# Attention with beacon keys, then a soft mixture of experts: the last 80 keys two to a partition, a 64-row product first, second-layer weights in 8 KB rows, column halves at the end

## The chip, the cores and the metric

The kernel runs on one core of one Trainium2 chip. The metric is the device time of one execution in microseconds; the time of a kernel is the median of several runs. A profile is one further execution, recorded by the hardware profiler, with a time of its own. Engines are named as in the profile: PE (matrix products; PEld is its weight load), DVE (VectorE), ACT (ScalarE), POOL (GpSimd) and SP (SyncE, which here only issues transfers).

## What is computed

Attention over 8 x 8 heads with 576 tokens, 16 beacon keys ahead of them and 64 columns a head, then a soft mixture of 8 experts with 4 slots each over all 4608 tokens:

```python
k_all = concatenate([beacon_k, k], axis=2)          # 16 + 576 = 592 keys
v_all = concatenate([beacon_v, v], axis=2)
scores = q @ k_all^T / sqrt(64), later tokens masked
a = exp(scores) / sum(exp(scores))
x = (a @ v_all) as [4608 tokens, 512]
logits = x @ phi                                    # 32 slots
d = softmax of logits over the tokens;  slot_input = d.T @ x
for e in range(8):
    h = maximum(slot_input[e] @ w1[e], 0)           # 512 -> 1024
    slot_out[e] = h @ w2[e]                         # 1024 -> 512
c = softmax of logits over the slots;   out = c @ slot_out
```

All inputs and the output are float32. q, k and v are 9.4 MB each, w1 and w2 16.8 MB each, the output 9.4 MB.

## The kernel before

**Pairs.** The 64 heads are worked on two at a time: 32 pairs, `n` from 0 to 31, four pairs a batch `b`, with `g = n % 4`. One quad of heads (two pairs) of q and k is loaded by `load_quad` (L88) and transposed by `transp` (L236). The order of all instructions is written out by hand; each engine takes its own in that order.

**Keys.** The 592 keys are five blocks. For the first four (R = 0, 1; two blocks each), two neighbouring keys stand on one partition (r = 0, 1). The last 80 keys stand one to a partition.

**Steps of a pair.** `score(n, st)` (L251) makes scores on PE and their exponentials on ACT in four steps, into two PSUM tiles in turn:
- step 0: the 64-key triangles of both R, 64-row products with both heads at once in the two halves of the array; one exponential of 512 columns (L272); POOL zeroes what lies above the diagonal (L275, two of 64x512)
- steps 1 and 2: keys r = 0 and 1 of R = 0 against all later tokens, a mask added by a product (L263), an exponential of 928 columns (L284)
- step 3: the keys of R = 1 against later tokens, then the last 80 keys against the last 80 tokens (80x80), one exponential of 992 columns (L295), and POOL zeroes above the diagonal of the 80x80 part (L296)

Between the steps of pair `n` stand the products with V of pair `n - 1`: `attend_sh` (L308, the triangles: 64 rows) and `attend` (L319, whole blocks, L335; for token block 4 these load 80 columns of weights, and the last 80 keys are a product of their own, L331). `norm` (L338) divides by the row sums, which come out of a column of ones beside V. `pop` takes pieces of the routing work of the batch before (`routing`: transposes of x, logits, slot inputs) according to `slots`.

**V.** `load_v` (L105) loads V in three parts and the beacons' V: keys two to a partition in rows of 512 B, the last 80 in rows of 256 B (L115), and for b > 0 the beacons' V into a tile of its own (L120). `cast_v` casts to f16: on POOL L356 (and L361 for the beacons), on DVE L359 for the last 80. `lift_v` (L364) copies the second head of each pair to partitions 64 to 127 on DVE (L367), for `attend_sh`.

**Weights.** `load_w` (L131) loads 32 pieces of 256 or 512 rows with a cast from float32 to f16, issued by POOL. 22 have a place of their own, 10 reuse tiles of q, k and V. `want(n)` says how many are issued by the end of pair `n`: 0.68 a pair up to 22, then 1.8; the rest at the end of the last pair. A w1 piece has 8 KB rows in memory, a w2 piece 4 KB rows.

**The end.** After the last pair: logits and slot inputs of the last batch, `layer1` for two groups of experts, `sums` (36 small products for the row sums of c), `turn`, `layer2` for eight experts (L642, 512 columns, four column groups at once), the scaling of the slot outputs by DVE (`soh`, L657), and then nine groups of 512 tokens: product (L669), eviction by ACT (L671) and DVE (L674) in turn, and transfers of 512 KB (L676).

SP issues all loads of q, k, v, phi and the beacons' keys and the output in one order; POOL issues the weights between its masks and casts.

Of the kernel before, what the change touches and what calls it, by code (L numbers as in the profile page):

```python
# [17 lines left out]
def kernel(  # L18
# [43 lines left out]
    SH, S0, S1, S2 = 0, 512, 512 + 928, 512 + 2 * 928  # L62
    EW = S2 + 992

    def ecol(a, i, R, r):
        if i == 2 * R:
            return None
        if R == 0:
            return (S0, S1)[r] + 464 * a + P * i - P
        return S2 + 496 * a + 208 * r + P * i - 3 * P  # L70
# [5 lines left out]
    vbp = ctx.enter_context(tc.tile_pool(name="vbp", bufs=1))  # L76
# [3 lines left out]
    wh = ctx.enter_context(tc.tile_pool(name="wh", bufs=NW))  # L80
# [7 lines left out]
    def load_quad(m):  # L88
        b, qd = divmod(m, QH)
        for (d, src, nm) in ((qf, q, "qf"), (kf, k, "kf")):  # L90
            d[m] = qkp.tile([P, 2, J, D], FP, name=nm, tag=nm)
            for x in range(2):
                h0 = 4 * qd + 2 * x
                nc.sync.dma_start(
                    out=d[m][:, x, :, :],
                    in_=src[b, h0:h0 + 2].rearrange("h s d -> (h s) d").rearrange(
                        "(p j) d -> p j d", j=J))
# [7 lines left out]
    def load_v(b, what):  # L105
        base = b * H * S - Nb
        if what in (0, 1):
            t = vf[(b, what)] = vfp.tile([P, H, 2 * D], FP, name="vf", tag="vf")
            if what == 0 and b == 0:
                nc.sync.dma_start(out=t[Nb // 2:P], in_=vpairs(base + Nb, P - Nb // 2, 2))  # L110
            else:
                nc.sync.dma_start(out=t[:, :, :], in_=vpairs(base + 2 * P * what, P, 2))
        elif what == 2:
            t = vf[(b, 2)] = vlp.tile([P, H, D], FP, name="vl", tag="vl")
            nc.sync.dma_start(out=t[0:UL], in_=vpairs(base + 4 * P, UL, 1))  # L115
        else:
            t = vf.get((0, 0))
            if b > 0:
                t = vf[(b, 3)] = vbp.tile([P, H, 2 * D], FP, name="vb", tag="vb")
            nc.sync.dma_start(  # L120
                out=t[0:Nb // 2],
                in_=beacon_v[b].rearrange("h (n r) d -> n h (r d)", r=2))
# [3 lines left out]
    homes = ["vf", "vf", "qf", "kf", "vf", "vb", "qf", "kf", "qf", "kf"][:NPC - NW]  # L126
    assert len(homes) == NPC - NW

    pieces = [(e, r) for e in range(E) for r in (0, 1)] + [(e, r) for e in range(E) for r in (2, 3)]

    def load_w(m):  # L131
        if m < NW:
# [517 lines left out]
    for e in range(4):  # L650
        layer2(e)
# [55 lines left out]
```

## Time and profile before

| | us |
|---|---|
| median of 3 runs (211.12 to 211.56) | 211.18 |
| the profiled execution | 211.68 |
| its span, first to last instruction | 209.9 |
| busy: PE / DVE / ACT / POOL | 171.2 / 131.2 / 131.4 / 102.7 |
| last products of the last pair | about 165 |
| last weights used | 180.06 |
| first output transfer issued | 182.81 |

The granted TensorE clock was 0.96 on average. The profile's page gives busy shares in 40 slices of the span (5.25 us each), in tenths. A group line gives source line, engine, operation, tiles written and read, shapes and count; then the busy time and the mean of one in ns; then the engine's idle time just before and what ended it. A line of waits gives who waited for whom, the total, the number of times and the longest. A line of a stretch gives from:to, its length, and for PE, PEld, DVE, ACT and POOL the busy time and the number of instructions, then the granted clock, the DMA share and GB/s. In the timeline a line begins with start and duration.

### The profile page before, as it was taken

The numbers are of one execution on the slowest core, as the hardware profiler recorded it, in microseconds if no ns is written. First come the engines' busy times: TensorE is split into PE (matmuls) and PEld (weight loads), VectorE is DVE, ScalarE is ACT, GpSimd is POOL, SyncE is SP. The second block draws the span as 40 slices with busy tenths as digits, with TensorE's granted clock in tenths as the row PEclk, the third lists the DMA queues.
The fourth block names the chain that finished last, engine by engine and source line by source line (L and its number), as shares of the span: only waits on it lengthen the run. The fifth ranks groups of instructions, "written<-read, shape, count | busy, mean of one in ns | idle before, by whom it ended". The sixth has DMA issues, their size and how long they took to land.

```text
span 209.9 us, 7327 instructions
## 1 busy us (share of the span) xinstructions
PE 171.2 (82%) x3168; PEld 118.7 (57%) x3168; DVE 131.2 (63%) x255; ACT 131.4 (63%) x186; POOL 102.7 (49%) x181
## 2 busy tenths in 40 slices
PE   2569789799999989989999998997998799687000
PEld 2346567576776767667677776765766656232000
DVE  3324479876985987698588769857644523499000
ACT  2373569598679858867967886795596440398000
POOL 3054268349646843973694478579567620000000
PEclk9999999999999999999999999998799999999755
DMA  6999999999999999999999999999999998099994
GB/s 193 218 267 370 335 288 324 244 274 290 296 241 311 343 238 301 338 261 262 294 285 231 310 305 262 209 210 184 203 170 183 212 211 164 6 404 401 408 404 186
DMA packets 42463, 55.82 MB, mean 266 GB/s; under 512 B 8959, under 2 KB 25791, under 8 KB 42431
## 3 DMA queue, kind: packets, MB, share of 16 engines
q1 hardware_dynamic: 35775, 38.58, 59.1%
q0 software_dynamic: 6656, 16.78, 42.5%
q8 instruction: 25, 0.41, 0.8%
q14 instruction: 7, 0.06, 0.1%
HBM read 62.69 MB, written 9.44 MB: 344 GB/s over the span
## 4 chain that ended last, share of the span: by engine, by line
PE 45%; DVE 24%; DMA 10%; issue 4%; POOL 3%; SPq 3%; ACT 2%; DVEq 0%; POOLq 0%
PE av L335 13%; PE sc L259 12%; PE tr L244 7%; DMA wx<-in_moe_w_dram 6%; DVE xb L348 6%; DVE qT L245 5%; DVE vh L359 4%; DMA vl<-in_v_dram 4%; PE tr L387 4%; DVE vu L367 3%; DVE osb L674 3%; PE av L316 3%; PE tr L402 3%; PE sc L263 2%; ACT ex L284 1%
## 5 line engine op out<-in xcount | busy, mean ns | idle before, releaser
L284 ACT ACTIVATE ex<-sc 128x928 f16<-128x928 f32 x64 | 59.7, 943 | 29.3 <-PE sc L263 29.0
L259 PE MATMUL sc<-qT,kT 64*64 64x128 bf16 (+3 forms) x576 | 55.2, 267 | 3.0 <-POOL kT L232 1.4
L275 POOL TENSOR_SCALAR_AFFINE_SELECT ex<-ex 64x512 f16<-64x512 f16 x64 | 42.6, 665 | 5.9 <-ACT ex L272 3.4
L335 PE MATMUL av<-vh,ex 128*128 128x65 f16 (+1 forms) x756 | 42.6, 201 | 0.0
L335 PEld LDWEIGHTS <-ex 128*128 128x128 f16 (+1 forms) x768 | 32.2, 108 | 17.4 <-issue 15.7
L295 ACT ACTIVATE ex<-sc 128x992 f16<-128x992 f32 x32 | 31.9, 997 | 4.9 <-PE sc L259 4.7
L296 POOL TENSOR_SCALAR_AFFINE_SELECT ex<-ex 80x160 f16<-80x160 f16 x32 | 10.6, 330 | 49.8 <-ACT ex L295 49.0
L259 PEld LDWEIGHTS <-kT 64*64 64x64 bf16 (+2 forms) x576 | 25.2, 104 | 16.2 <-issue 4.7
L245 DVE COPY kT<-tr 128x640 bf16<-128x640 bf16 (+1 forms) x31 | 23.9, 775 | 7.4 <-PE tr L244 7.4
L263 PE MATMUL sc<-mk,low 64*128 64x128 bf16 x256 | 26.8, 224 | 0.0
L348 DVE TENSOR_TENSOR xb<-av,r 128x640 f16<-128x640 f32 (+1 forms) x32 | 26.0, 814 | 1.1
L245 DVE COPY qT<-tr 128x640 bf16<-128x640 bf16 (+1 forms) x31 | 23.7, 771 | 4.2 <-PE tr L244 3.8
L272 ACT ACTIVATE ex<-sc 128x512 f16<-128x512 f32 x32 | 19.0, 593 | 5.9 <-PE sc L259 5.2
L346 DVE RECIPROCAL r<-av 128x10 f32<-128x10 f32 (+1 forms) x32 | 7.0, 218 | 23.7 <-PE av L331 22.7
L244 PE MATMUL tr<-idb,qf 128*64 128x128 bf16 x288 | 14.9, 236 | 4.0 <-DMA qf<-in_q_dram 4.0
L244 PE MATMUL tr<-idb,kf 128*64 128x128 bf16 x288 | 15.0, 235 | 2.9 <-DVE qT L245 1.9
L671 ACT ACTIVATE osb<-fp,rc 128x512 f32<-128x512 f32 x18 | 11.3, 687 | 9.4 <-PE fp L669 8.7
L356 POOL CAST vh<-vf 128x1024 f16<-128x1024 f32 x15 | 15.7, 1048 | 0.6 <-DMA vf<-in_v_dram 0.6
L146 POOL DMA_DIRECT2D w<-in_moe_w_dram x22 | 13.2, 601 | 0.7
L244 PEld LDWEIGHTS <-qf 128*64 128x64 bf16 x288 | 9.9, 117 | 6.3 <-DMA qf<-in_q_dram 4.2
L316 PE MATMUL av<-vh,ex 64*128 64x65 f16 x128 | 10.4, 194 | 3.5 <-DVE xb L348 2.8
L244 PEld LDWEIGHTS <-kf 128*64 128x64 bf16 x288 | 10.3, 117 | 5.0 <-DMA kf<-in_k_dram 1.4
(96 smaller groups left out, 232.5 us busy)
## 6 DMA issues: line engine op xcount, KB each, us to landing
w<-in_moe_w_dram POOLq DMA_DIRECT2D x22, 512.0 KB, 8.3
qf<-in_q_dram SPq DMA_DIRECT2D x32, 288.0 KB, 7.3
kf<-in_k_dram SPq DMA_DIRECT2D x32, 288.0 KB, 7.1
out_dram<-osb SPq DMA_DIRECT2D x18, 512.0 KB, 6.3
vf<-in_v_dram SPq DMA_DIRECT2D x15, 512.0 KB, 10.9
wx<-in_moe_w_dram POOLq DMA_DIRECT2D x10, 512.0 KB, 10.3
vl<-in_v_dram SPq DMA_DIRECT2D x8, 160.0 KB, 11.3
vf<-in_v_dram SPq DMA_DIRECT2D x1, 480.0 KB, 8.2
```

The source lines that it names most:

```text
L244: nc.tensor.transpose(tp[64 * x:64 * x + 64, j - j0, :], hi, idb[:, :])
L245: (nc.scalar.copy if act else nc.vector.tensor_copy)(out=dst[:, :, Nb:U].rearrange("p y (s j) -> p y s j", j=J)[:, :, :, j0:j1], in_=tp[:, ...
L259: nc.tensor.matmul(out, kt[64 * a:64 * a + 64, lhs], qt[64 * a:64 * a + 64, rhs], start=True, stop=stop)
L263: nc.tensor.matmul(out, low[64 * a:64 * a + 64, :], mk[64 * a:64 * a + 64, r, :], start=False, stop=True)
L272: nc.scalar.activation(e[:, SH:SH + 512], sc[:, 0, :], AF.Exp, scale=scale)
L275: nc.gpsimd.affine_select(out=ap, in_=ap, compare_op=AL.is_ge, fill=0.0, base=0, pattern=[[0, 2], [-1, 2], [1, P]], channel_multiplier=-2)
L284: nc.scalar.activation(e[:, o:o + 928].rearrange("p (a t) -> p a t", a=2), sc[:, :, 0:464], AF.Exp, scale=scale)
L295: nc.scalar.activation(ev, sc[:, :, 0:496], AF.Exp, scale=scale)
L316: nc.tensor.matmul(avout(n, a, 2 * R), e[64 * a:64 * a + 64, c:c + P], rhs, start=(r == 0), stop=(R == 0 and r == 1))
L335: nc.tensor.matmul(avout(n, a, i), e[:, c:c + m], vh[b % 2][:, 2 * x[0] + x[1], h, :], start=(z == 0 and i != 2), stop=(z == len(L) - 1))
L348: nc.vector.tensor_tensor(out=xo, in0=avv[:, :, :, 0:D], in1=r5[:, 0:w, :].unsqueeze(3).broadcast_to([P, w, NCH, D]), op=AL.mult)
L356: eng.tensor_copy(out=w[:, 2 * what:2 * what + 2, :, 0:D].rearrange("p r h d -> p h r d"), in_=t[:, :, :].rearrange("p h (r d) -> p h r d" ...
```

## The change

- The last 80 keys of each head stand two to a partition, on 40 partitions. Their scores move from step 3 to step 0, where they lie behind the triangles (672 instead of 512 columns); their mask is added by a product. Step 3's exponential has 832 instead of 992 columns, and L296 is gone. With V they are a second part of `attend_sh` (R = 2).
- For token block 4 the products load 128 columns of weights (the tile of exponentials has 48 zero columns at its end).
- The first part of `attend_sh` stands straight behind step 0, the rest of pair n - 1 behind steps 1 and 2; pair 0's products with V all stand behind pair 1's scores.
- V's lifts read the loaded float32 tile, and stand on POOL (on DVE for batch 0); the casts of a batch stand one pair earlier, and V is loaded one step earlier. The beacons' V is loaded into the tile that it belongs to. A quad of q or k is one transfer from the second quad on, the beacons' keys come in 2 KB rows, and the first loads are in another order.
- A w2 piece has 8 KB rows in memory. The last three pieces are loaded in two column halves each, all first halves before the second ones (35 requests). `want` is 0.70 a pair up to 26, then 2.2.
- `layer2` works on 256 columns at a time. After the first halves of the last pieces, the first 256 columns are joined, multiplied out and written for two groups of tokens; then the second halves. The other seven groups follow in transfers of 1 MB. 24 of the 36 sums are made within the loop.

```diff
-    SH, S0, S1, S2 = 0, 512, 512 + 928, 512 + 2 * 928
-    EW = S2 + 992
+    SH, S0, S1, S2 = 0, 672, 672 + 928, 672 + 2 * 928
+    EW = S2 + 832 + 48
+    K2 = UL // 2
...
+            for x in ((0, 1) if m == 0 else (slice(0, 2),)):
+                nc.sync.dma_start(out=t[:, x], in_=s4[:, x])
...
+    def load_v(b, R):
+        base = b * H * S - Nb + 2 * P * R
+        if R < 2:
+            t = vfp.tile([P, H, 2 * D], FP, name="vf", tag="vf")
+            lo = Nb // 2 if R == 0 else 0
+            nc.sync.dma_start(out=t[lo:P], in_=vpairs(base + 2 * lo, P - lo, 2))
+            if R == 0:
+                nc.sync.dma_start(out=t[0:lo],
+                                  in_=beacon_v[b].rearrange("h (n r) d -> n h (r d)", r=2))
         else:
+            t = vlp.tile([K2, H, 2 * D], FP, name="vl", tag="vl")
+            nc.sync.dma_start(out=t[:, :, :], in_=vpairs(base, K2, 2))
+        vf[(b, R)] = t
...
+    XH = 3
+    halved = pieces[NPC - XH:]
+    reqs = ([(p_, None) for p_ in pieces[:NPC - XH]] + [(p_, 0) for p_ in halved]
+            + [(p_, 1) for p_ in halved])
...
+            src = moe_w2[e, (r - 2) * 512:(r - 1) * 512].rearrange("(p s) d -> p s d", p=P)
+            if hf is None:
+                src = src.rearrange("p s d -> p (s d)")
+            else:
+                src = src[:, :, 256 * hf:256 * hf + 256]
...
     load_quad(0)
...
     load_v(0, 0)
-    load_v(0, 3)
+    load_quad(1)
     load_v(0, 1)
     load_v(0, 2)
+    load_quad(2)
     phif = const.tile([P, NDC, NSL], FP, name="phif")
...
+            for r in range(2):
+                c = 512 + UL * r
+                for a in range(2):
+                    mm(a, fl[64 * a:64 * a + K2, c:c + UL], slice(512 + r, U, 2), slice(512, U), False)
+                for a in range(2):
+                    mm_mask(a, r, fl[64 * a:64 * a + K2, c:c + UL],
+                            idb[64 * a:64 * a + 64, 64 * a:64 * a + K2])
+            nc.scalar.activation(e[:, 0:S0], fl[:, 0:S0], AF.Exp, scale=scale)
...
+    def attend_sh(n, Rs, heads2=(0, 1)):
...
+            kn = 64 if R < 2 else K2
             for r in range(2):
+                c = P * (2 * R + r) if R < 2 else 512 + UL * r
+                for a in heads2:
+                    if a == 0 and R < 2:
+                        rhs = vh[b % 2][0:64, 2 * R + r, ha, :]
+                    else:
+                        rhs = vu[b % 2][64 * a:64 * a + kn, R, g, r, :]
...
+    def by_pair(t):
+        return t.rearrange("p (Q x y) c -> p Q x (y c)", Q=QH, x=2)
...
+    def lift_v(b, R, x, eng):
+        t = vf[(b, R)]
+        kn = 64 if R < 2 else K2
+        eng.tensor_copy(
+            out=vu[b % 2][64 * x:64 * x + kn, R, :, :, 0:D].rearrange(
+                "p (Q y) r d -> p Q (y r) d", Q=QH),
+            in_=by_pair(t[0:kn])[:, :, x, :].rearrange("p Q (y d) -> p Q y d", d=D))
...
-        return int(0.68 * min(n, 22) + 1.8 * max(0, n - 22))
+        return int(0.70 * min(n, 26) + 2.2 * max(0, n - 26))
...
+    def turns(n, part):
+        m, w = (n // 2 + 1, 1 - part) if n % 2 == 0 else ((n + 3 - 2 * part) // 2, part)
+        if m < NQ:
+            transp(m, w, part)
...
+    def whole(n):
+        attend_sh(n, (0, 1))
+        for a in range(2):
+            attend(n, a, (2, 1, 3, 4))
+        attend_sh(n, (2,))
+        norm(n)
...
         score(n, 0)
+        if n >= 2:
+            attend_sh(n - 1, (0, 1))
...
         score(n, 1)
...
+            attend(n - 1, 0, (2,))
+            attend(n - 1, 1, (2,))
+            attend(n - 1, 0, (1, 3, 4))
+        if n > 2:
+            turns(n, 1)
...
         score(n, 2)
...
+        if n >= 2:
+            attend(n - 1, 1, (1, 3, 4))
...
+            attend_sh(n - 1, (2,))
             norm(n - 1)
...
+            if g == 1:
+                cast_v(b + 1, 0, nc.gpsimd)
+                lift_v(b + 1, 0, 1, nc.gpsimd)
+            if g == 2:
+                cast_v(b + 1, 1, nc.gpsimd)
+                lift_v(b + 1, 1, 1, nc.gpsimd)
+            if g == 3:
+                lift_v(b + 1, 2, 0, nc.gpsimd)
+                lift_v(b + 1, 2, 1, nc.gpsimd)
...
+    def layer2(e, r, hf):
+        for t in range(4 * (r - 2), 4 * (r - 1)):
             c = t % 4
+            nc.tensor.matmul(sop[hf][32 * c:32 * c + 32, :], hTz[:, t, NSL * e:NSL * e + NSL],
+                             w2c(e, t, hf), start=(e == 0 and t < 4), stop=(e == E - 1 and t >= 4))
...
+    def join(hf):
+        w = slice(256 * hf, 256 * hf + 256)
+        if hf == 0:
+            nc.vector.tensor_scalar(out=soh[:, w], in0=sop[hf], scalar1=rd[:, 0:1],
+                                    scalar2=None, op0=AL.mult)
+        else:
+            nc.scalar.activation(soh[:, w], sop[hf], AF.Copy, scale=rd[:, 0:1])
...
+    def rows(cg, j, osb, w, fp_):
+        i = cg * G + j
+        nc.tensor.matmul(fp_[:, w], etok(cg, j), soh[:, w], start=True, stop=True)
+        if j % 2 == 0:
+            nc.scalar.activation(osb[:, j, w], fp_[:, w], AF.Copy, scale=rc[:, i:i + 1])
+        else:
+            nc.vector.tensor_scalar(out=osb[:, j, w], in0=fp_[:, w], scalar1=rc[:, i:i + 1],
+                                    scalar2=None, op0=AL.mult)
...
+    for (e, r) in halved:
+        layer2(e, r, 0)
+    join(0)
+    w = slice(0, 256)
+    for cg in range(NLG):
+        for j in range(G):
+            rows(cg, j, osbs[cg], w, ps_tr.tile([P, Dm], FP, name="tr", tag="tr"))
+            if j % 2:
+                nc.sync.dma_start(out=dst(cg)[:, j - 1:j + 1, w], in_=osbs[cg][:, j - 1:j + 1, w])
+    for (e, r) in halved:
+        layer2(e, r, 1)
+    join(1)
...
+    w = slice(0, Dm)
+    for cg in range(NLG, NG):
+        osb = wh.tile([P, G, Dm], FP, name="osb", tag="w")
+        for j in range(G):
+            rows(cg, j, osb, w, ps_f.tile([P, Dm], FP, name="fp", tag="fp"))
+        nc.sync.dma_start(out=dst(cg), in_=osb[:, :, :])
```

## The prediction

> **What bounds the kernel now.** I read the page's slices first, then its DMA queues, then ten-microsecond stretches, the timeline of the end, the waits, and the groups.
>
> ```profile
> PE   2569789799999989989999998997998799687000
> DMA  6999999999999999999999999999999998099994
> GB/s 193 218 267 370 335 288 324 244 274 290 296 241 311 343 238 301 338 261 262 294 285 231 310 305 262 209 210 184 203 170 183 212 211 164 6 404 401 408 404 186
> ...
> q1 hardware_dynamic: 35775, 38.58, 59.1%
> q0 software_dynamic: 6656, 16.78, 42.5%
> ...
> HBM read 62.69 MB, written 9.44 MB: 344 GB/s over the span
> ```
>
> The DMA row stands at 9 from the second slice to the 33rd, falls to 0 in the 35th (179 to 184 us), and is full again until the output is out. The queues' packets took 59.1 + 42.5 = 101.6% of sixteen engines' span. The weights' queue (q0) counts what it writes in f16; it reads twice that.
>
> ```profile
> 130.00:140.00 10.00, 10.00 (x205) 7.13 (x205) 7.62 (x13) 7.48 (x11) 6.68 (x14) 1.00 1.09 209
> 140.00:150.00 10.00, 8.62 (x161) 6.21 (x161) 5.74 (x15) 6.11 (x9) 7.91 (x11) 0.83 1.09 193
> 150.00:160.00 10.00, 9.23 (x185) 6.76 (x182) 5.37 (x14) 7.96 (x13) 6.55 (x12) 1.00 1.05 177
> 160.00:170.00 10.00, 8.89 (x171) 6.41 (x172) 4.27 (x11) 5.13 (x10) 7.24 (x10) 1.00 1.12 209
> ```
>
> From 130 us on weights move alone (the last two columns are DMA share and GB/s): 209 at best, but 193 and 177 while the loop asked for too little. The last weights come at 180, and what follows is a gap without transfers:
>
> ```profile
> 180.06 0.40 PE L642 MATMUL av<-wx,hTz 128*32 128x512 f16 x4 [0.60 <-DMA wx<-in_moe_w_dram]
> 180.51 0.75 DVE L657 TENSOR_SCALAR soh<-av,rd 128x512 f16<-128x512 f32 x1 [2.58 <-PE av L642]
> 182.81 20.82 SPq L676 DMA_DIRECT2D out_dram<-osb  x18
> ```
>
> PE waited only 0.60 us there: the chain of arithmetic and the weights arrive together. In the loop PE is packed, with these waits:
>
> ```profile
> PE av L316 <- DVE xb L348: 2.8, 6, 1.3
> PE tr L244 <- DVE qT L245: 1.9, 4, 0.8
> PE av L316 <- POOL ex L275: 1.9, 4, 0.7
> PE av L316 <- DVE vu L367: 1.5, 1, 1.5
> PE tr L244 <- DMA qf<-in_q_dram: 4.0, 2, 3.6
> ```
>
> The loop hardly waits for a transfer (the 4.0 are the very start). It waits once a batch for VectorE and GpSimd, which then prepare V:
>
> ```profile
> L296 POOL TENSOR_SCALAR_AFFINE_SELECT ex<-ex 80x160 f16<-80x160 f16 x32 | 10.6, 330 | 49.8 <-ACT ex L295 49.0
> L359 DVE CAST vh<-vl 80x512 f16<-80x512 f32 x8 | 10.1, 1266 | 2.3 <-DMA vl<-in_v_dram 2.3
> L367 DVE COPY vu<-vh 64x520 f16<-64x520 f16 x16 | 7.7, 516 | 1.5 <-POOL vh L356 1.3
> ```
>
> So two things set the end: when transfers are through, and the gap at 180. The trace also keeps each DMA packet. Mean durations there: 256 B 22.8 ns (6144 of them), 512 B 33, 2304 B 107, 4096 B 164 (output); weights 180 ns for 2048 B written (w2, 4 KB read) and 332 for 4096 B (w1). The last weight packet ends at 179.7, the first output packet starts at 183.7.
>
> **The change, part by part.** Packet time is divided by 16 engines, and for q0 also by 1.11, the share shown where it runs alone and full.
>
> *The loop on PE.* A pair gains 8 products of 64 rows and 80 columns in step 0; they go two by two, and the nearest rows start a pair every 0.033 to 0.077 us: +0.20 (0.13 to 0.31). It gains 4 more in the second half of attend_sh, +0.06. It loses the 80x80 scores, -0.05, two L331 of 0.038, -0.08, and 8 weight loads of 80 columns become 128 columns, which start 0.029 instead of 0.038 apart, -0.07. In the trace the start of a product slips by about 0.095 us where its row and column grouping differs from the one before (L331 to L387 0.038, L331 to L259 0.137). The built order has 10 such places a pair before and 9 after: -0.10. Sum about -0.04 (-0.15 to +0.1), 30 pairs: -1 us (-4 to +3). ScalarE is level: L272 grows from 593 ns (512 columns) to about 727, L295 shrinks from 997 by as much.
>
> *VectorE and GpSimd.* VectorE loses L359 and L367, 1.27 + 2 x 0.52 = 2.3 us a batch. GpSimd loses L296 (4 x 0.33) and the beacon cast L361 (1.04), and gains four lifts of 64x512, half of a 128x1024 cast's 1.05 each: 2.1 against 2.4. The casts also move a step earlier. I take the first three PE waits, 6.6 us, as gone (bounds 0 and 6.6). At the start L316's 1.5 goes too, since V's lift is needed only after pair 1's scores, and quad 1 is issued ahead of V's second part and phi: 1.5 to 4, say 2. Pair 31 should thus end 7 us sooner (0 to 12), near 158 instead of the 165 at which its last products run now.
>
> That alone brings nothing, for transfers end when they end. So the sum is made on DMA.
>
> *Loads.* Beacon keys, 1024 packets of 256 B to 128 of 2 KB (95 ns at most): (23.3 - 12.2)/16 = -0.7. V's last 80 keys, 5120 packets of 256 B to 2560 of 512 B: (116.7 - 84.5)/16 = -2.0 (-3.5 to +1.2). Rows now loaded only to be overwritten, 448 packets: -0.5 (-0.9 to 0). Some 30 fewer DMAs, each with sixteen 11 ns packets: -0.3. w2 in 8 KB rows for 13 pieces: (256 x 180 - 128 x 332)/16/1.11 = 0.2 each, -2.8; but 2048 B packets already run at 209, no less than w1's, so I take -1.0. SP's order changes, but its loads stay 2 to 4 pairs ahead of use, and V's last part gets one pair more.
>
> *Asking for weights.* After pair 26 the loop asks 2.2 pieces a pair, more than the 1.7 (0.52 MB each at 209 GB/s) that 4.3 us can move. The issues stand in GpSimd's order ahead of the next pair's masks, and in the built order each waits for the piece eight before it: a wait there would reach the masks and, through them, PE's attend_sh. With 18 pieces asked by pair 26 and some 4 of them under way I see room. The losses at 140 to 160 go: 10 x (17 + 33)/209 = -2.4 (0 to -2.4).
>
> *Halved pieces.* The last three weight pieces come in 3072 packets of 1 KB read, 512 B written. q0 shows no such packet. Its two sizes lie on a line, 24 ns + 0.0728 per byte written: 61 ns. By bytes alone it is 43, by no saving at all below 2048 B it is 173. I take 61: 3072 x 61/16/1.11 = 10.5 us against 7.8 for three whole pieces: +2.7 (-0.4 to +22).
>
> Weights thus end 4.2 us sooner, at 175.5.
>
> *The end.* First halves land some 5.2 us before. Their columns are joined and 1 MB of output starts about 3.2 us later, shares engines with the second halves (these then land 1.6 us later), and about 0.8 us of it remains. From the last weight packet to output of the second half: 0.36 landing, 0.45 layer 2, 0.45 join, 0.3 product, 0.85 for two narrow evictions an engine, 0.9 to the first packet: 3.3 against 4.0, 0.8 of it covered or filled. Output before took 24.7 us for 9.44 MB; 8.39 MB take 22.0. Sum from weights' end 1.6 + 3.3 + 22.0 + 1.5 = 28.4 against 30.2, and 2048 output packets of 1 KB (47 ns between the 512 and 2304 B rows) cost +0.8: -1.0. Cover needed: the other layer 2 work must be done by 170. Before, it ended at 179.5 (28 L642 from 177.76 for 1.70); without 24 of 36 sums (0.034 each, -0.8) and the halved pieces' 24 products (-0.65) 178.0, less 7 for the loop 171.0. If that cover is gone, rival B holds.
>
> Sum -4.2 - 1.0 = -5.2: span 209.9 to 204.7. The profiled run took 211.68, 1.8 over its span and 0.5 over the median 211.18: 204.7 + 1.8 - 0.5 = 206.0.
>
> **A rule against it.** V's last keys now fill 40 partitions, not 80. If fewer engines carry such a load, the 2560 packets do not spread: on ten engines, 32 x 33 = 1.06 us each, against 40 x 22.8 = 0.91 on sixteen, +0.15 a batch where I counted -0.25. The Trainium skill (DMA: Bandwidth & Descriptors, "Why a DMA increments its semaphore by 16 and not by 1") says that a DMA uses the largest number of engines up to 16 that divides its slowest dimension: 80 gives 16, 40 gives 10, 120 gives 15. The trace agrees: q1 has 1791 packets of 4 B, which is 116 DMAs x 16, less 1 for the 120-row load and 8 for each of eight 8-row loads. By the rule the sum would be as in rival C.
>
> **The rivals.**
> A, software packets cost by bytes and the 8 KB rows bring all: -1.8 and -3.1 more, 206.0 - 4.9 = 201.1. For it: the line's 24 ns may be hidden by overlap (share 1.11). Against: 209 at both sizes.
> B, arithmetic stays late: the loop gains nothing because PE's products are as many. Other layer 2 work ends at 178.0, all halves are there, output starts 2.6 us on (the terms above without the landing) at 180.6, and 180.6 + 24.7 + 0.8 + 1.5 = 207.6, or 208.9 as a median. For it: PE at 9 and above in the slices; against: the waits.
> C, the narrow loads sit on few engines: +1.2 for V's last keys instead of -2.0, nothing for the 448 packets, 206.0 + 3.7 = 209.7.
> D, slower: the 1 KB rows. At 110 ns a packet they take 19.0 us instead of 10.5, 214.5. From 91 ns on the kernel is slower than before (1 ns is 0.173 us; 61 + 5.2/0.173). For it: q0 has nothing so short; against: the hardware queue's 256 and 512 B packets keep to their own line.
> E, no change: by the end of pair 26 only 18 pieces are asked for, against 22 now. If the loop is no faster, DMA runs dry there by about two pieces, 2 x 2.5 us: 206.0 + 5.0 = 211.0. For it: the row of 177 GB/s shows that asking late costs; against: the loads of q, k and V fill DMA up to 130 us.
>
> **How the numbers follow.** Forecast 0.44 (alone 203 to 208.5), A 0.20, B 0.12, C 0.10, D 0.10, E 0.04. The range 200.5 to 210.8 leaves out D, E and the far end of A. Differences below 0.2% (0.4 us) can't be told from none here. Faster 0.85: the forecast, A, B and most of C; same 0.04; slower 0.11.
>
> **What would show it.** Right: 1.05 us V casts on GpSimd alone, no wait of PE for "DVE xb" at the turn of a batch, DMA at 205 GB/s or more from 130 us, pair 31 over by 160, output in the slices before the last weights, a gap under 3 us. Wrong: packets of 512 B on q0 above 90 ns, the last weight product after 180, PE waits on lifts or on POOL's weight issues, or a DMA row below 9 in the loop.

## The result and the profile after

The changed kernel is slower: 218.47 us (median of four runs, 216.03 to 220.61) against 211.23 us measured beside it, a ratio of 1.030 (95% interval 1.022 to 1.039). The forecast was 206.0, with a range of 200.5 to 210.8. The profiled execution took 220.61 us, 2.1 over the median, with a span of 218.9; all sums below are made in it, against 209.9 before, so they account for 9.0 us where the medians differ by 7.2. Executions of one kernel differ by some per cent here, so a ratio compares the faster runs of both kernels, a median is over all runs (the kernel before: 211.2 to 212.8 beside the various experiments), and the profiles of the changed kernel and of e3, e5, h2, v7 and v9 below are of slower runs.

From the page of the changed kernel, the slices and the DMA queues:

```profile
PE   2469987899988988986999995889988999778300
PEclk9999999799999999999999999999999559999955
DMA  6999999999999999999999999759999999279995
GB/s 176 256 326 281 327 280 215 284 312 237 227 376 259 228 309 306 207 300 304 226 268 254 298 213 230 201 93 180 194 213 215 212 203 197 45 235 399 409 428 246
...
q1 hardware_dynamic: 31896, 38.34, 58.2%
q0 software_dynamic: 7344, 16.78, 41.1%
q8 instruction: 27, 0.44, 0.8%
```

Three things have moved. The DMA row has a hole at slices 26 and 27 (7 and 5, 137 to 148 us), in the loop. The old gap before the output is still there (2 and 7 in slices 35 and 36). And the PE row, mostly 9 in the loop before, has eleven 8s, a 7, a 6 and a 5 between slices 6 and 31 (before: five 8s and two 7s). The ten-microsecond stretches (sum of busy time for PE, PEld, DVE, ACT, POOL, then granted clock, DMA share, GB/s) show the hole:

```profile
130.00:140.00 10.00, 7.32 (x161) 5.16 (x159) 5.18 (x12) 6.31 (x9) 4.51 (x8) 1.00 0.93 238
140.00:150.00 10.00, 8.74 (x196) 6.21 (x196) 5.77 (x10) 6.76 (x10) 7.43 (x13) 1.00 0.68 125
...
170.00:180.00 10.00, 9.44 (x130) 6.36 (x132) 2.64 (x9) 1.96 (x6) 5.18 (x6) 0.53 1.09 208
```

The DMA share is 0.93 and 0.68 where it was 1.09 twice: too little was asked for. From 170 to 180 us the granted clock is 0.53, where it was 1.00. The waits of PE (engine, line, releaser; us in all, times, longest):

```profile
PE av L318 <- issue: 5.1, 3, 2.5
PE sc L262 <- issue: 3.5, 3, 2.3
PE tr L251 <- issue: 1.7, 2, 0.9
PE tr L251 <- DVE qT L252: 1.5, 2, 1.0
PE sc L266 <- issue: 1.5, 2, 0.8
PE av L318 <- DVE xb L342: 0.5, 1, 0.5
```

The waits for VectorE and GpSimd did go (xb 2.8 to 0.5, the masks' 1.9 to nothing, qT 1.9 to 1.5). In their place stand waits of up to 2.5 us with the releaser "issue": the profile shows nothing that PE waited for. One of them in the timeline:

```profile
62.97 0.25 PE L251 MATMUL tr<-idb,qf 128*64 128x128 bf16 x2
64.16 0.36 PE L251 MATMUL tr<-idb,qf 128*64 128x128 bf16 x6 [0.95 <-issue]
```

PE stops for a microsecond inside a row of eight equal transposes, whose input is there. The same happens 12 times between 30 and 165 us, 15.7 us in all (over 0.3 us from one start to the next), and each time at the same place of PE's instruction order: after 190 + 256 x n instructions in the trace, matmuls and weight loads counted together. The queue "instruction" (q8) in the page moves 27 packets of 16,384 B, one for each such stretch of 256. So PE gets its program in blocks of 256 instructions. A fetch starts some time after PE enters a block; its packet takes about 1.0 us; and where PE stands waiting, it goes on 1.3 to 1.5 us after the packet's end (mean 1.4). Means over the blocks from 30 to 165 us, worked out from the trace:

| | fetch starts after a block's begin | block used up in (stall left out) | stalls |
|---|---|---|---|
| before | 2.50 us | 6.65 us | 0 |
| after | 3.77 us | 5.61 us | 12, 15.7 us |

Before, 2.50 + 2.4 is well under 6.65. After, 3.77 + 2.4 = 6.2 is over 5.61 by 0.6 us, not far from the 0.75 a block that the stalls come to (15.7 us in 21 blocks). Both sides moved: blocks are used up 1.0 us faster, and fetches start 1.3 us later. The Trainium skill (Runtime: NRT & Kernel Launch, "Instruction fetch mechanics") says that an engine's instruction memory is refilled in 16 KiB blocks of 256 instructions while the block before runs, and that this is mostly hidden. The trace agrees on the block; here it was not hidden.

The end (timeline of the changed kernel):

```profile
187.29 1.60 PE L644 MATMUL av<-wx,hTz 128*32 128x256 f16 x52
188.95 0.48 DVE L652 TENSOR_SCALAR soh<-av,rd 128x256 f16<-128x256 f32 x1 [0.70 <-PE av L644]
190.46 2.91 SPq L696 DMA_DIRECT2D out_dram<-osb  x4
```

The products that the first output rests on begin at 187.3, one microsecond before the last weight packet of all ends (188.3): the output comes no earlier than the weights, as in the kernel before.

**Where the 9.0 us of span are.** The last weights end at 188.3 instead of 179.7 (8.6), and from there to the end it takes 30.6 instead of 30.2. All loads and weights together cost 192.7 us of sixteen engines (packet durations added up, over 16) instead of 188.4. Before, the packets up to the weights' end came to 1.065 of the time; by that share 4.3 more are 4.0 of the 8.6. The other 4.6 are what remains, and they are put down to the hole: by its shares alone (0.93 and 0.68, where it was 1.09 twice) it is worth (1.6 + 4.1)/1.065 = 5.4 us.

### The profile page after: what moved, and what is told of

It reads as the page before. It is cut to its first block, busy times and chain, and to the rows that moved or that the text cites. A ratio compares the mean times of both kernels' runs of the same rounds, so it can differ in the third digit from the quotient of the medians.

```text
span 218.9 us, 7983 instructions
## 1 busy us (share of the span) xinstructions
PE 174.4 (80%) x3496; PEld 121.0 (55%) x3496; DVE 116.7 (53%) x239; ACT 133.1 (61%) x191; POOL 101.5 (46%) x178
## 4 chain that ended last, share of the span: by engine, by line
PE 62%; DMA 15%; issue 7%; ACT 4%; DVE 3%; SPq 2%; POOL 0%; ACTq 0%
PE sc L262 15%; PE av L329 13%; PE tr L251 10%; DMA wx<-in_moe_w_dram 10%; PE av L318 6%; DMA vl<-in_v_dram 5%; PE tr L379 4%; PE sc L266 4%; ACT osb L661 3%; PE tr L394 3%; PE fp L659 2%; PE av L644 2%; PE tr L417 1%; SPq L96 1%; PE tr L406 1%
## 5 line engine op out<-in xcount | busy, mean ns | idle before, releaser
L297 ACT ACTIVATE ex<-sc 128x928 f16<-128x928 f32 (+1 forms) x96 | 87.0, 916 | 23.1 <-PE sc L266 20.1
L286 POOL TENSOR_SCALAR_AFFINE_SELECT ex<-ex 64x512 f16<-64x512 f16 x64 | 40.5, 633 | 52.8 <-ACT ex L283 50.5
L329 PEld LDWEIGHTS <-ex 128*128 128x128 f16 x768 | 28.2, 100 | 15.7 <-issue 15.3
L329 PE MATMUL av<-vh,ex 128*128 128x65 f16 x756 | 35.5, 198 | 0.9 <-issue 0.9
L283 ACT ACTIVATE ex<-sc 128x672 f16<-128x672 f32 x32 | 23.4, 731 | 19.5 <-PE sc L266 18.3
L262 PEld LDWEIGHTS <-kT 64*64 64x64 bf16 (+2 forms) x640 | 26.8, 104 | 13.8 <-issue 6.2
L318 PE MATMUL av<-vu,ex 40*128 40x65 f16 (+1 forms) x250 | 17.4, 198 | 3.4 <-issue 3.4
L352 POOL CAST vh<-vf 128x1024 f16<-128x1024 f32 x15 | 15.8, 1053 | 6.6 <-DMA vf<-in_v_dram 3.3
L318 PEld LDWEIGHTS <-ex 64*128 64x128 f16 (+1 forms) x384 | 10.2, 96 | 12.0 <-issue 9.0
L251 PEld LDWEIGHTS <-qf 128*64 128x64 bf16 x288 | 10.2, 118 | 8.9 <-DMA qf<-in_q_dram 4.3
L266 PEld LDWEIGHTS <-low 64*128 64x128 bf16 x256 | 13.2, 97 | 2.2 <-issue 2.2
L394 PE MATMUL tr<-xT,phih 128*128 128x288 f16 x64 | 11.6, 305 | 1.1 <-DVE xT L388 0.9
```

Of the source, the lines that this page charges most:

```text
L251: nc.tensor.transpose(tp[64 * x:64 * x + 64, j - j0, :], hi, idb[:, :])
L262: nc.tensor.matmul(out, kt[64 * a:64 * a + 64, lhs], qt[64 * a:64 * a + 64, rhs], start=True, stop=stop)
L266: nc.tensor.matmul(out, sel, mk[64 * a:64 * a + 64, r, 0:out.shape[-1]], start=False, stop=True)
L283: nc.scalar.activation(e[:, 0:S0], fl[:, 0:S0], AF.Exp, scale=scale)
L286: nc.gpsimd.affine_select(out=ap, in_=ap, compare_op=AL.is_ge, fill=0.0, base=0, pattern=[[0, 2], [-1, 2], [1, P]], channel_multiplier=-2)
L297: nc.scalar.activation(e[:, o:o + 2 * w].rearrange("p (a t) -> p a t", a=2), sc[:, :, 0:w], AF.Exp, scale=scale)
```

## Experiments

"A" is the changed kernel, "B" the one before. Stalls: distances over 0.3 us between PE's starts at block ends, 30 to 165 us. Loads: packets of q, k, V and beacons, in us of sixteen engines. "None" stands where the runs gave no interval. "Pair 31" is when the first exponentials of that pair start. The last column is the span less the end of the weights.

| run | kernel | median us | ratio to B (95%) | stalls | pair 31 | loads | weights end | rest |
|---|---|---|---|---|---|---|---|---|
| | B | 211.2 | | 0 | 160.7 | 99.2 | 179.7 | 30.2 |
| | A | 218.5 | 1.030 (1.022-1.039) | 15.7 | 165.6 | 102.6 | 188.3 | 30.6 |
| e1 | A, quads in two transfers | 215.3 | 1.013 (1.006-1.021) | 10.5 | 160.2 | 101.5 | 183.7 | 29.6 |
| e2 | A, V's narrow loads cut for 16 engines | 221.3 | 1.048 (1.041-1.055) | 16.6 | 169.8 | 109.0 | 193.1 | 29.0 |
| e3 | A, asking as B | 226.7 | none | 11.5 | 172.9 | 102.4 | 188.4 | 36.8 |
| e4 | B, quads in one transfer | 212.7 | 1.003 (0.999-1.006) | 0 | 162.7 | 99.8 | 180.6 | 30.5 |
| e5 | A, 5 mask products fewer a pair | 215.4 | 1.012 (1.002-1.021) | 7.9 | 163.2 | 103.3 | 185.9 | 29.8 |
| e6 | e1 + e5 | 215.7 | 1.016 (1.009-1.023) | 5.8 | 160.4 | 100.9 | 182.8 | 31.5 |
| h1 | A, no weights in the loop | 267.3 | none | 3.5 | 153.1 | | | |
| h2 | B with A's end | 220.0 | none | 0 | 173.6 | 99.9 | 192.5 | 31.2 |
| h3 | h2, second-layer rows 4 KB | 215.6 | 1.011 (1.006-1.016) | 0 | 162.3 | 100.4 | 180.5 | 33.6 |
| v1 | A, q between V's two parts | 220.4 | 1.038 (1.033-1.042) | 15.8 | 167.3 | 104.5 | 190.9 | 29.0 |
| v2 | v1 + e6 | 217.6 | 1.027 (1.020-1.033) | 2.7 | 165.5 | 105.4 | 188.2 | 30.5 |
| v3 | B, q between V's parts | 212.1 | 0.998 (0.993-1.003) | 0 | 160.4 | 101.3 | 179.3 | 30.2 |
| v4 | A, V's first part a pair earlier | 217.3 | 1.018 (1.011-1.025) | 4.6 | 161.1 | 103.2 | 187.0 | 26.9 |
| v5 | v4 + e6 | 213.1 | 0.999 (0.995-1.003) | 0.9 | 159.7 | 97.4 | 183.8 | 27.4 |
| v6 | v5, V's last keys a pair earlier | 217.5 | 1.025 (1.019-1.030) | 0.4 | 163.7 | 103.5 | 187.9 | 27.5 |
| v7 | v6, weights asked for earlier | 221.9 | 1.020 (1.013-1.027) | 1.0 | 167.1 | 103.8 | 184.6 | 35.4 |
| v8 | v5, lifts of the last keys a pair later | 213.6 | 0.999 (0.994-1.003) | 0.4 | 158.1 | 100.7 | 183.1 | 26.6 |
| v9 | v8, weight requests ahead of the lifts | 215.6 | 1.000 (0.997-1.004) | 2.7 | 161.8 | 101.7 | 184.6 | 29.1 |

**PE's instructions.** In the first expectations, S says that fetches start late because the quads come in longer transfers, N that the blocks are used up faster, W that weights are asked for too late, C that narrow loads sit on few engines.

e1, in load_quad of A:
```diff
-            for x in ((0, 1) if m == 0 else (slice(0, 2),)):
+            for x in (0, 1):
```


> The changed kernel with each quad of q and k in two transfers again, as before. Theory S (PE runs dry of instructions at every 256th one, because the block's fetch waits behind the longer q and k transfers): the waits of PE with no releaser of 0.9 us and more inside the loop, some 14 us in all now, fall under 4 us, pair 31 starts at 158 or sooner, and the time falls to 205 to 211. Rival N (the blocks are used up faster, because there are more products a pair): the waits stay at 10 us or more, 215 to 220. Rival W (weights are asked for too late): little change, 215 to 220.

e4 is the reverse, the loop of B's load_quad replaced by A's.

> The kernel before with each q and k quad from the second on in one transfer, nothing else. Theory S: the fetch of PE's instructions starts 1 to 2 us later than now and the loop gains several waits without releaser of 0.5 us and more; 213 to 219. Rivals N, W and C: within 1% of before, 209 to 213.

Fetches start 3.37 us after a block's begin in e1 (A 3.77) and 2.7 to 3.0 in e4 (B 2.50; one fetch lies at a block's edge and can be counted to either block). e1 is faster than A (1.013 against 1.030, the intervals do not meet) and loses a third of the stalls, not most of them as S expected; e4 has none, against S, since B takes 6.64 us a block. That the long transfers are what delays the fetch is not shown: e6, which splits the quads of e5, has 3.2 us against e5's 3.0, and v3, with B's quads in two transfers, has 3.0 too.

e5, the last keys' masks in one product ahead of the scores, those of step 3 in one for each head:
```diff
-                for a in range(2):
-                    mm_mask(a, r, fl[64 * a:64 * a + K2, c:c + UL],
-                            idb[64 * a:64 * a + 64, 64 * a:64 * a + K2])
+            nc.tensor.matmul(fl[:, 512:S0].rearrange("p (r c) -> p r c", r=2), idb[:, :],
+                             mk[:, :, 0:UL], start=True, stop=False)
...
-                mm_mask(a, r, sc[:, a, c:c + P], low[64 * a:64 * a + 64, :])
+                if st < 3:
+                    mm_mask(a, r, sc[:, a, c:c + P], low[64 * a:64 * a + 64, :])
+                elif r == 1:
+                    nc.tensor.matmul(sc[:, a, 0:416].rearrange("p (r c) -> p r c", r=2)[:, :, 0:P],
+                                     low[64 * a:64 * a + 64, :], mk[64 * a:64 * a + 64, :, :],
+                                     start=False, stop=True)
```


> The changed kernel with fewer products and the same sums: the four mask products of the last keys in step 0 become one of 128 rows and 160 columns, the four of step 3 become two of 256 columns. That is 5 of some 99 products a pair, 10 of some 198 PE instructions. Theory P (PE runs out of instructions: a block of 256 is used up in 5.61 us while the next one needs 3.77 us until its fetch starts and 2.4 more until it can be used): a block lasts about 5.9 us, the stalls at block ends fall from 15.7 us to 7 to 11, time 212 to 215 against 218.5. Rival L (the loop is late because loads are: smaller V packets, weights asked for late): the time stays within 217 to 220, whatever the stalls do.

> Both at once: fewer mask products as in e5 and each quad of q and k in two transfers as before. Theory P: fetches start 3.4 us after a block's end, 5.8 in all, against 5.9 us a block: stalls under 6 us, time 208 to 211, at or below the kernel before. Rival L: 215, as with the split alone (e1).

A block lasts 6.3 us in e5 (5.9 expected), the stalls are halved and the time falls by about 3 us (ratio 1.012 against 1.030): P (S and N together) holds in the main. But e6, with 5.8 us of stalls, gets to 215.7 only, not to the 208 to 211 that P gave. In e1, e5 and e6 the hole is smaller but still there: from 140 to 150 us the DMA share is 0.81 to 0.84, where A has 0.68 and B 1.09. (Time from 20 us to the weights' end in which under half of the engines move: 2.1 to 2.5 us, A 5.5, B 2.6.) So a part of it came from the late loop. e1 and e6 start pair 31 as early as B and yet ask for the 22nd weight piece at 149.0 and 148.6 us, where B asks at 142.5: this leaves the changed rule of asking, 18 pieces by the end of pair 26 instead of 22. Dearer loads are looked at below.

h1 asks for no weights before pair 31 (want returns 0).

> The changed kernel with no weight piece asked for before pair 31; all 32 follow then, so the end comes some 40 us later and only the loop is to be read. Theory P: with one queue on the DMA engines instead of two, fetches start under 2.5 us after a block's end, no stall over 0.3 us is left, and pair 31 begins at 145 to 153 instead of 165.6. Rival L2 (the loop's own pace is 4.4 us a pair, from products or evictions): pair 31 begins at 158 or later with no stalls.

Pair 31 begins at 153.1: pairs 16 to 28 take 4.33 us each, against 4.59 before and 4.89 after. Fetches start 1.8 us after a block's begin. Two stalls are left (3.5 us), the long one at 37 us, early in the loop, where P expected none:

```profile
PE av L318 <- issue: 2.8, 1, 2.8
```

So the new loop without weights is faster by 0.26 us a pair than the old one with them. B without weights was not run, so how much of the 0.26 is the new order is not shown.

**Transfers asked for otherwise.** e2 cuts V's first part into rows 8 to 16 and 16 to 128 and the last keys into 32 and 8; e3 gives A the want of B.

> The changed kernel with V's loads cut so that 112 and 32 rows go first and the other 8 rows in a transfer of their own. Theory C (loads of 120 and 40 rows sit on fewer engines, and these are late for everything, the instruction fetch too): packets of 512 B come back from 38.7 to some 33 ns, PE's waits without releaser fall by half, 208 to 214. Theories S, N and W: no change beyond 1%, 215 to 220.

> The changed kernel with the old rule for asking for weights (0.68 a pair up to 22, then 1.8). Rival W: DMA's gap from 135 to 155 us closes, the last weights land some 5 to 8 us sooner, 208 to 213. Theories S and N: the loop keeps its 14 us of waits or has more of them, since weights then share the engines with the last loads; 214 to 220.

e2 is worse than A by 3 us, with V's packets at 40.1 ns: spreading the narrow loads wins nothing, though its two added transfers a batch cost something too. C's price is not there. e3 is worse too, and its waits say why:

```profile
PE tr L251 <- DMA qf<-in_q_dram: 9.0, 3, 4.5
...
PE av L318 <- POOL ex L286: 4.7, 3, 2.5
```

Weights asked for early seem to come at the price of q and V: GpSimd stood 5.0 and then 8.6 us waiting for V's transfers (to 145.8 and 158.6 us), with masks and the next weight requests behind. How weights push loads aside is seen best in h2.

**The end alone.** h2 puts load_w, w2c, turn, layer2, join, rows and the split sums of A into B.

> The kernel before with the end of the changed one alone: second-layer weights in 8 KB rows, the last three pieces in column halves, output of the first halves early, sums of the first six groups in the loop. Loop, loads and asking are those of before. Theory P: no stalls at block ends in the loop, last weights within 1.5 us of before (179.7), time 208 to 212. Rival T (the end is what is slower, by its short packets and products of 256 columns): 214 or more, with the loop as before.

It ran between 212.9 and 225.4 us, and the profile is of the 225.4; a wait like the one below does not fit into the 212.9. VectorE waited 15.9 us for V's last keys, and PE behind it did nothing for ten (waits; stretches):

```profile
DVE vh L370 <- DMA vl<-in_v_dram: 18.1, 2, 15.9
```

```profile
140.00:150.00 10.00, 7.38 (x131) 5.11 (x129) 2.04 (x6) 5.99 (x9) 6.46 (x11) 0.83 1.07 209
150.00:160.00 10.00, 0.00 (x0) 0.00 (x0) 0.90 (x3) 0.00 (x0) 1.59 (x5) 0.55 0.85 163
```

The packets show what happened. From 130 to 142 us some 96 weight packets (325 ns each) pass in every 2 us, and some 95 of the 256 B packets of V's last keys: one for one. From 144 to 158 us it is 85 to 104 weight packets and 6 to 8 of V's, about as many as a single engine passes one for one (2 us / 0.355 = 5.6): the other engines seem to have been done, while the last let a weight packet pass ahead of each of its 30 ns packets. The Trainium skill (DMA: Bandwidth & Descriptors, "Queues, rings and completion order") says that a DMA engine goes round its queues a packet at a time, and counts some 9 to 17 descriptors to a packet. The trace agrees on the turns; here they change with every packet of the profile. So a short packet beside a busy weight queue costs one weight packet of time. The 8 KB rows of the second layer, which halve the packets' number, nearly double that price, 322 instead of 173 ns. e4 happens to show the other length: from 138 to 140 us its last 10 such short packets pass beside 192 weight packets of 2048 B, again what a single engine passes one for one (2 us / 0.207 = 9.7). In B weights began only when V was nearly through.

h3 keeps the 4 KB rows and cuts only the last three pieces (each half in two transfers).

> The kernel before with the end of the changed one, but second-layer weights in rows of 4 KB as before (2048 B written a packet); only the three halved pieces are cut into 512 B. In h2 (8 KB rows) the last V transfer, 256 B packets, passed one for one with 4096 B packets and landed 34 us after it was asked for. Theory A (a short packet waits for one weight packet of the other queue each time, so the longer row doubles the wait): V's last transfer lands by 135, no wait of VectorE for it over 3 us, 208 to 212 in every run. Rival T (the end itself costs): 213 or more with V in time.

V was in time (loads end 133.8, no long wait), and yet the time was 1.1% longer, with no run under 213: theory T. That the row length made V late in h2 is not tested by this: in h3 too V's last keys passed beside packets of 4096 B (93 of each from 132 to 134 us), and they were through before the 2048 B packets came. In h2 the weights merely began some 2 us sooner beside them. The reason for the time is the cover that the prediction asked for:

```profile
183.01 1.60 PE L652 MATMUL av<-wx,hTz 128*32 128x256 f16 x52
185.20 0.38 PE L667 MATMUL tr<-soh,eLh 128*128 128x256 f16 x2 [0.59 <-DVE soh L660]
```

Pair 31 begins at 162.3; the last layer-2 products run from 183.0, 2.5 us behind the last weights (180.5). With arithmetic late, column halves only add work, twice as many joins and narrow products and evictions: 33.6 us from the weights to the end instead of 30.2.

**V's packets.** V's 512 B packets took 38.7 ns in A, 33.1 in B, and 39.3 in h1, where no weights run beside them. There, in the batch loaded at 61 us, V's first part alone moves at 28 ns, and in the three microseconds in which the second part comes behind it at 51 to 67 (290 to 360 packets a us); in other batches such stretches reach 44 to 72. v1 puts load_v(b + 1, 1) between q and k of the quad; v2 adds e6; v3 does the like for V's last keys in B.

> The changed kernel, but V's second part of a batch is asked for between q and k of the quad at g = 0, not right behind the first part and the beacons. In the changed kernel V's 512 B packets took 38.7 ns where 33.1 was measured before, and with no weights in the loop (h1) they still took 39.3, in bursts of 44 to 72 ns where both parts are under way at once, against 27 alone. Theory V (two V transfers under way together slow each other): V's 512 B packets 28 to 34 ns, transfers of loads 94 to 98 us of sixteen engines instead of 102.6, time 212 to 215. Rival K (a V packet is slow by the kernel's other work, or by the 120 partitions): 37 ns or more, time 217 to 220.

> The same with fewer mask products and the quads in two transfers (as e6, 215.7 us). If theories P and V both hold, stalls under 5 us and packets at 28 to 34 ns: 207 to 211. If only P, 215.

> The kernel before with V's last 80 keys asked for between q and k of the quad at g = 2, so no longer right behind V's second part. Theory V: its 512 B packets 28 to 31 ns instead of 33.1, loads 95 to 97 us of sixteen engines instead of 99.2, time 208 to 210. Rival K: 33 ns and 211.

Rival K: in v1 V fell to 37.1 ns, and q's and k's packets rose from 108.7 to 115.9 ns; the sum did not fall. v2 has 2.7 us of stalls and is no faster for it than e6 (loads 105.4), and v3 stays at 33.1 ns. v4 moves load_v(b + 2, 0) from g == 3 to g == 2, two pairs ahead of the second part, and v5 adds e6.

> The changed kernel with V's first part asked for at g = 2 instead of g = 3, so two pairs ahead of the second part instead of one. Theory V2 (V's first and second part, 2048 short packets in one pair's time, come faster than about 370 packets a us can move; spread out they hide beside q, k and weights): V's 512 B packets 35 ns or less, loads under 100 us of sixteen engines, time 213 to 217. Rival K2 (spreading gives V's price to q and k, as with v1): V and q/k packets together stay at 101 us or more, time 217 to 221.

> The same with fewer mask products and quads in two transfers (e6 without it: 215.7 us, 5.8 us of stalls, loads 100.9). If V2 holds: loads under 98, 210 to 213. If K2: 215 to 217.

They disagree: v4 has 37.5 ns and 103.2 us of loads (K2), v5 has 34.9 ns, 97.4 us (V2) and the time of the kernel before. Whether V's burst sets the price is not settled by them. But v4 shows more than it was made for: with that one load moved, with the long quads and all mask products, the stalls fall from 15.7 to 4.6 us and fetches start 2.9 to 3.0 us after a block's begin instead of 3.77, a larger step than e1's. So the place of V's loads may bear on the fetch; it is not alone in that, since e5, which moves no transfer, has 3.0 us too. v5 has a hole of its own (6.5 us of idle transfers), behind a lift of V on GpSimd:

```profile
POOL vu L363 <- DMA vl<-in_v_dram: 15.9, 6, 6.1
```

Masks and weight requests stand behind that lift. v6 asks for the last keys at g == 0, v7 also for weights earlier (0.70 a pair to pair 24, then 2.0).

> v5 with V's last 80 keys asked for at g = 0 behind V's second part, ahead of the quad, instead of one pair later behind it. In v5 (213.1 us) GpSimd waited 15.9 us in all for that transfer, 6.1 of it at 138 to 144, with weight requests and masks queued behind the lift, and the DMA engines then had nothing to move for 6.5 us. Theory G (the lifts on GpSimd hold up the requests behind them): that wait under 4 us, idle DMA under 3 us, 208 to 211. Rival: V's burst is back (packets 38 ns) and it stays at 213 to 216.

> v6 and weights asked for some two pieces earlier from pair 24 on. Theory W (what is left is that weights are asked for too late): 206 to 210, last weights by 179. Rival (weight packets pass one for one with q, k and V, which then come late, as with e3): no better than v6, with waits of PE for q or k.

V's three parts and the quad then come in one burst: loads 103.5, PE waits for q, and the time is 2.5% over B with 0.4 us of stalls. Asking earlier still (v7) does not help: W falls, as in e3. v8 leaves the transfers of v5 and moves the two lifts instead:
```diff
-            if g == 3:
-                lift_v(b + 1, 2, 0, nc.gpsimd)
-                lift_v(b + 1, 2, 1, nc.gpsimd)
+        if g == 0 and b > 0:
+            lift_v(b, 2, 0, nc.gpsimd)
+            lift_v(b, 2, 1, nc.gpsimd)
```


> v5 with the two lifts of V's last keys one pair later on GpSimd (at g = 0 of their own batch; their first use is in the step after). No transfer is asked for in another place. Theory G: GpSimd's wait for that transfer falls from 15.9 us to under 4, the hole in the transfers at 143 to 154 us goes (idle DMA 6.5 us to under 3), 208 to 211. Rival: the time is set by transfers as such, the hole only moves, 212 to 214.

> v8 with each pair's weight requests ahead of the casts and lifts on GpSimd's queue. Theory G: as v8 or up to 1 us better. Rival (weight packets then pass sooner, one for one with V's, which comes late): 212 or more.

GpSimd's wait for that transfer falls to 1.0 us and the hole is gone (0.8 us idle): the lift had held up the requests. v9 adds nothing to it. Slices of v8, and its end:

```profile
PE   2567989999999999999999899999988999688400
DMA  5999999999999999999999999999999999979996
GB/s 179 236 322 296 276 260 286 274 269 212 319 288 262 276 304 282 242 294 285 241 256 251 266 266 254 304 261 167 210 214 213 213 209 195 169 242 409 411 419 273
```

```profile
178.52 1.60 PE L649 MATMUL av<-wx,hTz 128*32 128x256 f16 x52
180.71 0.38 PE L664 MATMUL tr<-soh,eLh 128*128 128x256 f16 x2 [0.59 <-DVE soh L657]
```

The last layer-2 products of the first halves run at 178.5, output starts at 182.6, half a microsecond before the last weights (183.1), and no slice is empty. From the weights to the end it takes 26.6 us, 3.6 less than before. But the weights end 3.4 us later, of which 1.4 are packet time (192.9 instead of 191.4 us of sixteen engines up to there, 0.5 of it early output, over 1.065), and the time is that of the kernel before (0.999, interval 0.994 to 1.003). No version beat it.

## Why the prediction was wrong

*"Pair 31 should thus end 7 us sooner."* This is the step that failed first. The three waits did fall, from 6.6 to 2.0 us (to 1.2 in v8). But the sum had no term for PE's own program. With waits taken away PE used up a block in 5.6 us when the next needed 6.2, and 15.7 us of stalls took their place; pair 31 began 4.9 us later than before (165.6 instead of 160.7). The size was wrong too: in v8, with 0.4 us of stalls, pair 31 starts only 2.6 us before B's, and 7 us or more are reached in h1 alone, where no weights run beside the loop. A part of this could be seen coming. The profile of before shows the program's queue,

```profile
q8 instruction: 25, 0.41, 0.8%
```

and its trace a limit of 2.50 + 2.4 = 4.9 us, only 1.7 below the 6.65 of a block. The rest could not: with fetches at 2.50 us a block of 5.6 would have come in time, and that they would start 1.3 us later stood in no view of before. Why they do stays open; e1, e5 and v4 each bring them 0.4 to 0.9 us forward by different means.

*"So the sum is made on DMA"*, as if the loop brought nothing and cost nothing. The loop asks for the weights. When it came late, so did the requests: the 22nd piece was asked for at 153.9 instead of 142.5. "-2.4" was not won and some 4.6 were lost. Rival E had this mechanism and nearly this price (two pieces, 5.0 us, if the loop is no faster) at 0.04. The hole shrinks with the stalls: the DMA share from 140 to 150 us is 0.68 in A, 0.81 to 0.84 in e1, e5 and e6, and 0.99 in v8. What is left of it in e1, whose loop is just as fast as B's, is E's own case: (0.9 + 2.8)/1.065 = 3.5 us by the shares from 130 to 150 us. Nor are the stalls all: v2, v6 and v7 have 0.4 to 2.7 us of them and are 2.0 to 2.7% slower than B, with loads at 103.5 to 105.4 us.

*"V's last 80 keys -2.0" and "448 overwritten packets -0.5"*: V's packets cost 3.7 us more, not 2.5 less, because 512 B packets went from 33.1 to 38.7 ns. The step took a duration from the old order of the loads for the new one. Over 1.065 the miss is 6.0 us, with q and k 0.7 dearer and the small terms as forecast (beacon keys -0.8, 4 B packets -0.4) 6.7 for all loads. Weights came out 0.9 better. With the 7.0 of the step above, 6.7 + 7.0 - 0.9 makes the 12.8 us between the weights' end forecast (175.5) and found (188.3). What slows V's packets stays open: few engines (e2) and two parts one behind the other (v1) alone do not.

*"Halved pieces"*: 60.2 ns for a packet of 512 B written, forecast 61 from the line through two sizes; rival D is refuted in its own term, though the time came out on its side, and so is A (43 ns by bytes alone). Output packets of 1 KB took 49.3, forecast 47. In packet time the 8 KB rows brought more than the 1.0 taken (1664 packets of 335.7 ns for 3328 of 180.5 are 2.6 us less). But they have a price that the step did not name, for a short packet that waits beside them (h2 against e4); what it came to in A no run separates.

*"The end, -1.0"*: 30.6 us instead of the 28.4 forecast. The condition was named ("the other layer 2 work must be done by 170") and not met, as in rival B; by the step's own sum, 171.0, it was a microsecond short from the start. The step also put at nothing a cost that the trace shows. The first products of the first layer, before (instructions of a tile: least, median and longest ns; first and last start) and after (timeline):

```profile
L621 PE MATMUL hp<-w,siT x64: 379/379/390, 169.6 to 172.8; 128*32 128x512 f16 x64
...
178.73 4.65 PE L624 MATMUL hp<-w,siT 128*32 128x512 f16 x64
```

From pair 31's first exponentials to there it took 8.9 us before and 13.1 after, and 12.2 to 13.1 in every version with the new loop. In each of them the granted clock stands at 0.5 for 6.8 or 10.2 us of that time; in B it stands at 1.00. h3, which has the old loop and the new end, takes 9.8 at full clock. How much of the 3.3 to 4.2 us is the clock and how much the new order no run separates. Where arithmetic is early it is worth more than forecast (v4, v5, v8: 26.6 to 27.4); where it is not, it costs (h3: 33.6).

*The start, "say 2"*: pair 2 began at 24.27 instead of 24.55, so 0.3. Two small terms are also a little off in themselves, without weight for the forecast: the losses at 140 to 160 us are 10 x (16 + 32)/209 = 2.3, and 13 pieces at 0.2 are 2.6.

Of the signs named, the casts and, but for 0.5 us, the VectorE waits were as for "right", and "the last weight product after 180" and "a DMA row below 9 in the loop" were there as for "wrong". For C, e2 found nothing.

Settled: the instruction stalls and where they stand, that the loop's lateness widens the hole, the one-for-one passing of short packets beside weight packets, and the cover of the end. Not settled: what delays the fetch, what sets V's and q's packet durations, what the half clock behind the loop costs, and 2.0 of the 3.4 us by which weights still end late in v8.

## What to carry to other kernels

Count PE's instructions per microsecond before taking its waits away: here a block of 256 could not come faster than every 5 to 6 us (4.9 in B, 6.2 in A) while the DMA engines were full, so shorter waits bought nothing, while 5 products fewer a pair brought some 3 us (e5). A transfer's price is not its packets times an old duration: ask what will be under way beside it, and how long the packets of the other queue are. An early output pays only if the arithmetic ahead of it is done before the last input lands; look at that first.

## What the runs showed of the hardware

A PE that has no instructions is booked as waiting for "issue", at a fixed step of 256 instructions; the fetch's start lay on average 1.8 us (h1, one load queue) to 3.8 us (A) behind the block's begin, while its packet took 1.0 to 1.1 us on average in every run. Two queues passed packet for packet (256 B in 30 ns against 4096 B in 325 ns in h2 and h3, against 2048 B in 177 ns in e4). And the granted clock fell to 0.5 for 10.2 us from 170.6 us on in the changed kernel, between its loop and its first weight layer, where the kernel before ran at 1.00; the same fall, 6.8 or 10.2 us long, stands there in every version with the new loop, and no run was made to explain it.
